# Block 0's last-row values turned on TensorE instead of through DRAM, and fillers between the late output-weight units

## The chip, the cores and the metric

The kernel runs on one core of one Trainium2 chip. A core has five engines with an instruction queue each: PE (TensorE, matrix multiplication), ACT (ScalarE), DVE (VectorE), POOL (GpSimd) and SP (SyncE, which issues most DMAs here). The data lies in SBUF, 128 partitions wide; TensorE writes into eight PSUM banks. The metric is the device time of one execution in microseconds (us), lower is better. Before the change it is 850.03 us, the median of three runs (849.67 to 851.71).

## The reference

A recurrent, memory-augmented attention layer with 32 heads, then a layer-normalised MLP. Shapes: 2048 tokens, width 512, 32 heads of 128, segments of 32 tokens, 8 memory rows.

```python
mem = mem0                                     # 8 x 512
for s in range(64):                            # 64 segments of 32 tokens
    xs = layernorm(x)[:, 32*s:32*s+32]
    h  = concatenate([mem, xs], axis=1)        # 40 rows
    q, k, v = (einsum('btd,dhe->bhte', h, W) for W in (Wq, Wk, Wv))
    scores = where(mask, einsum('bhqe,bhke->bhqk', q, k) * 128**-0.5, -1e9)
    o = einsum('bhqk,bhke->bhqe', softmax(scores), v)
    o = einsum('bhte,hed->btd', o, Wo)         # output projection
    mem = o[:, :8]                             # feeds the next segment
    outs.append(o[:, 8:])
h  = x + concatenate(outs, axis=1)
out = h + (gelu(layernorm(layernorm(h)) @ w1 + b1) @ w2 + b2)
```

The mask is causal, except that the 8 memory columns are open to all rows. Each segment needs the memory rows that the one before it made, so the 64 segments are one chain.

## The kernel before

Weights stay in SBUF: `WQ`, `WK`, `WV`, `WO` are 4 MB each, in bfloat16. They are loaded at the start: WV, WK, WQ as four DMAs of 1 MB, WO as sixteen of 256 KB, in this order on SP's queue. The Python list `chain` holds the order (`load` appends to it, and each DMA of the list comes behind the one ahead of it on SP).

The 40 rows of a segment are split. 32 of them, 8 memory rows and the first 24 token rows, are the "A" part (`hT`), which must wait for the memory. The last 8 rows of four successive segments together make a "B" part of 32 rows (`hB`), one per block of four segments, which needs no memory and is projected ahead of time. A projection pass (line 744, or 490 where the weights are kept) takes four 128-row steps; four matmuls of 512 columns run side by side in one step, in four column groups of the array. Passes come in halves r = 0 and 1, of 16 heads each.

The values of the B part come out as `VSB`: its partition stands for (column group j, segment s of the block, row t), and the four heads i of a group lie beside each other in the columns. For the product with the probabilities it is needed the other way round: in `VBD` the partition stands for (j, i, t), and the four segments s lie in the columns. Before the change `v_B_spread` (lines 832 to 844) does that through DRAM: four DMAs write `VSB` to the scratch tensor `v_last` (line 836), and four more read it back into `VBD` in 512-byte pieces (line 842). For block 0 these eight DMAs stand in the list of loads: `spread["out", 0]` behind WV and WK, `spread["in", 0]` behind WQ and the first two of WO's sixteen.

```python
chain[14:14] = spread["in", 0]
chain[8:8] = spread["out", 0]
```

`VSB` is a single buffer. Block 1's values (the entry `("B", "V", 1, ...)`) can be copied into it only when block 0's have been read. Such dependences are kept by tile: the class `Sched` records every operation with what it reads and writes, ranks them by estimated durations, and puts each engine's operations into an order; semaphore waits follow from it. TensorE's order is the one in which the code takes its operations: for segment 0 the hand-written list `START`, for the others `ORDER`. In `START`, `"X"` is the layer norm of token block 1 with its transposes, `"WO"` the output projection of segment 0, held back, and `("T", "WO", a, b)` takes its units a to b - 1. There are eight units (line 1009), and unit q needs the WO loads 2q and 2q + 1. Behind the last unit, DVE turns the result (line 1021) and adds halves into the memory columns of `hT` (line 1015), with which segment 1's projections begin.

TensorE's instruction stream is padded: `align` counts instructions and puts weight loads without a matmul (LDWEIGHTS, line 742) into the projections at a segment's start, so that the stream reaches a chosen place in its blocks of 256 (`PHASE`).

Of the kernel before, what the change touches and what calls it, by code (L numbers as in the profile page):

```python
# [44 lines left out]
START = (("B", "V", 0, (0, 6), (1, 7)), "V", "X", ("B", "V", 1, (0, 6), (1, 7)), ("B", "K", 0, (0, 4), (1, 6)), "K0", "K1", ("B", "K", 1, (0, 4), (1, 6)),  # L45
         ("B", "Q", 0, (0, 5)), "Q0", ("B", "Q", 0, (1, 4)), "Q1", "Z", "SC0", "SC1", ("B", "Q", 1, (0, 5)), "PV0", "PV1", "SA", "WO", ("T", "WO", 0, 3),
         ("B", "Q", 1, (1, 6)), ("T", "WO", 3, 8))


class Op:  # L50
# [394 lines left out]
P = 128  # L445
# [6 lines left out]
H = 32  # L452
# [9 lines left out]
MC, MR, MF = 1, 2, 3  # L462
# [45 lines left out]
def build_kernel(nc, A_x, A_mem0, A_Wq, A_Wk, A_Wv, A_Wo, B_w1, B_b1, B_w2, B_b2, out):  # L508
    scale = float(E) ** -0.5
    S = Sched(nc)  # L510
    st = contextlib.ExitStack()
    with st:
# [6 lines left out]
        WO = sb("WO", [P, H, D])  # L519
# [9 lines left out]
        ident = sb("ident", [P, P])  # L529
# [13 lines left out]
        VSB = sb("VSB", [P, 4, 2, E])  # L543
        VBD = sb("VBD", [P, 2, 4, 2, E])
# [14 lines left out]
        OTB = sb("OTB", [P, 2, H, 32])  # L559
# [55 lines left out]
        for sl in range(2):  # L615
            for i in range(4):
# [20 lines left out]
             reads=["maskA"], writes=["maskA"])  # L637
# [120 lines left out]
        def copy2(out, src, n, ps_=True, scale_=None):  # L758

            fast = 1.0 if ps_ else 0.5  # L760
            if scale_ is None:
                return {"act": (lambda e: e.copy(out, src), t_act(n, ps_)), "dve": (lambda e: e.tensor_copy(out, src), 0.16 + 1.042e-3 * n * fast)}  # L762
            return {"act": (lambda e: e.mul(out, src, scale_), t_act(n, ps_)),  # L763
                    "dve": (lambda e: e.tensor_scalar(out, src, scale_, None, ALU.mult), 0.16 + 1.042e-3 * n * fast)}
# [52 lines left out]

        def v_B_out(bk, r, bank):
            S.either(copy2(VSB[:, :, r, :], ps[bank][:, :].rearrange("p (i e) -> p i e", i=4), 512), reads=[("ps", bank)], writes=[("VSB", r)])
            if r == 1:  # L820
                v_B_spread(bk)

        def kq_B(bk, qk, r, bank, back=False):
# [4 lines left out]
        def v_B(bk, r, bank, back=False):  # L828
            one_pass(*pack_b(bk), WV, "WV", r, bank, cols_v, back)
            v_B_out(bk, r, bank)  # L830

        def v_B_spread(bk):

# [352 lines left out]
        for s in range(NS):  # L1186
# [109 lines left out]
            if s == 0:  # L1296

                for n in START:
                    if n[0] == "B":
                        _, what, b, *halves = n  # L1300
                        for r, bank in halves:
                            if what == "V":
                                v_B(b, r, bank)
                            else:
                                kq_B(b, "KQ".index(what), r, bank)
                    elif n[0] == "T":
                        S.take((0, n[1]), n[2], n[3])
# [157 lines left out]
```

## Time and profile before

| | us |
|---|---|
| median of three runs | 850.03 |
| the profiled execution's own time | 852.85 |
| its span, first to last instruction | 851.0 |
| PE busy | 801.9 (94%) |
| DVE, ACT, POOL busy | 566.5, 553.2, 265.3 |
| DMA packets, moved | 66615, 48.80 MB |

The span is the time between the first and the last instruction of the profiled execution; the rest of its time lies around it. All places below are given in us from the span's start. "PE" stands for matmuls, "PEld" for weight loads, "SPq" for the work of SP's queue, which issues DMAs; "PEclk" is the clock that was granted to TensorE, as a share of full speed. A row such as `[1.10 <-DMA WO<-in_A_Wo_dram]` says that the engine stood idle for 1.10 us before the instruction, and what ended the idleness. A segment takes about 10.5 us of the span in the steady part, and the first segment's work, with the loads, fills the first 52 us.

### The profile page before, as it was taken

The page shows a single profiled execution, that of the slowest core. Times are in us where ns is not written, and L with a number is a line of the kernel's source. Part 1 is how long each engine was busy: PE and PEld are TensorE (multiplying, and loading weights), DVE is VectorE, ACT ScalarE, POOL GpSimd, SP SyncE. Part 2 cuts the span into 40 slices and gives each one's busy share as a digit, 9 for nine tenths or more (in the row PEclk, how much of TensorE's full clock was granted, in tenths as well). Part 3 has the DMA queues.
Part 4 walks back from the last instruction along what each step waited for, and adds up shares of the span by engine and source line. Part 5 has one row for each costly group of instructions (what it writes and reads, how often), then busy time and mean ns, then how long its engine had stood idle before and what let it go on. Part 6 is the DMA issues. An engine that isn't in the chain of part 4 may idle for free.

```text
span 851.0 us, 47411 instructions
## 1 busy us (share of the span) xinstructions
PE 801.9 (94%) x20061; PEld 438.9 (52%) x22307; DVE 566.5 (67%) x1818; ACT 553.2 (65%) x1561; POOL 265.3 (31%) x686
## 2 busy tenths in 40 slices
PE   3668999999999999999999999999999998999998
PEld 1245555555555555555555555555555555544443
DVE  3257677878787878777778777777777776633111
ACT  2446777767776767777777777777777776742442
POOL 5023114242424242424242333323232313166200
PEclk9979999999999999999999999999999999999999
DMA  9961000110101010101010101010112121274100
GB/s 344 361 193 22 10 17 22 30 29 23 35 20 38 17 40 16 35 22 35 23 35 22 35 23 35 17 29 17 28 35 54 47 72 35 70 195 111 50 25 25
DMA packets 66615, 48.80 MB, mean 57 GB/s; under 512 B 29156, under 2 KB 62828, under 8 KB 66412
## 3 DMA queue, kind: packets, MB, share of 16 engines
q1 hardware_dynamic: 66080, 45.50, 18.4%
q8 instruction: 166, 2.72, 1.3%
q10 hardware_dynamic: 332, 0.27, 0.1%
q14 instruction: 37, 0.30, 0.1%
HBM read 31.34 MB, written 8.39 MB: 47 GB/s over the span
## 4 chain that ended last, share of the span: by engine, by line
PE 84%; DMA 5%; DVE 3%; POOL 3%; SPq 2%; issue 2%; ACT 1%; ACTq 0%; POOLq 0%; DVEq 0%
PE ps L744 36%; PE ps L1009 13%; PE ps L490 10%; PE quad L1357 6%; PE ps L1350 4%; PE ps L1036 4%; PE quad L919 3%; PE quad L977 3%; DMA oN<-opT 2%; PE quad L889 2%; PE ps L947 2%; PE ps L1164 2%; POOL opT L1050 2%; SPq L671 1%; DMA xr<-in_A_x_dram 1%
## 5 line engine op out<-in xcount | busy, mean ns | idle before, releaser
L762 ACT CAST OT<-quad 128x128 bf16<-128x128 f32 (+1 forms) x192 | 85.2, 444 | 144.8 <-PE quad L977 86.5
L970 POOL COPY BD<-PTA 32x192 bf16<-32x192 bf16 x256 | 88.8, 347 | 245.7 <-DVE PTA L966 222.7
L1009 PE MATMUL ps<-WO,OT 128*32 128x256 bf16 x4224 | 130.5, 275 | 4.5 <-DMA WO<-in_A_Wo_dram 3.7
L744 PE MATMUL ps<-WV,hT 128*32 128x512 bf16 x1780 | 132.7, 381 | 0.0
L744 PE MATMUL ps<-WQ,hT 128*32 128x512 bf16 x1796 | 123.3, 385 | 5.8 <-DVE hT L1015 4.4
L762 ACT CAST kq<-ps 128x512 bf16<-128x512 f32 x160 | 92.5, 588 | 34.0 <-PE ps L744 32.1
L1009 PEld LDWEIGHTS ps<-WO,OT 128*32 128x32 bf16 x4224 | 107.1, 97 | 12.9 <-DMA WO<-in_A_Wo_dram 3.7
L744 PE MATMUL ps<-WK,hT 128*32 128x512 bf16 x1544 | 108.8, 385 | 0.0
L763 ACT ACTIVATE kq<-ps 128x512 bf16<-128x512 f32 x160 | 92.6, 600 | 21.1 <-PE ps L744 20.8
L742 PEld LDWEIGHTS <-hT 128*32 128x32 bf16 x3942 | 65.8, 98 | 59.3 <-DVE hT L1015 30.8
L785 DVE STREAM_TRANSPOSE KALL<-kq 128x256 f32<-128x256 f32 x160 | 69.0, 438 | 24.1 <-ACT kq L762 14.6
L901 ACT ACTIVATE EC<-quad,nmc 128x64 f32<-128x64 f32 x252 | 77.2, 313 | 2.5 <-DVE nmc L897 0.2
L762 ACT CAST VS<-ps 128x512 bf16<-128x512 f32 x127 | 74.4, 586 | 0.0
L960 DVE TENSOR_REDUCE sma<-SA 128x8 f32<-128x256 f32 x64 | 26.9, 420 | 71.1 <-ACT SA L959 71.1
L744 PEld LDWEIGHTS ps<-WK,hT 128*32 128x32 bf16 x1544 | 45.9, 97 | 43.3 <-issue 24.6
L785 DVE STREAM_TRANSPOSE QT<-kq 128x256 f32<-128x256 f32 x128 | 55.7, 435 | 18.7 <-ACT kq L763 17.4
L806 POOL COPY ZC<-QTB 128x256 bf16<-128x256 bf16 x64 | 25.3, 396 | 122.8 <-PE quad L889 63.3
L1353 ACT ACTIVATE WQ<-ps,b1t 128x512 bf16<-128x512 f32 x42 | 28.9, 688 | 51.9 <-PE ps L1350 51.9
L919 PEld LDWEIGHTS quad<-PTC,VS 32*128 32x128 bf16 x2048 | 24.1, 91 | 74.0 <-ACT EC L901 24.3
L744 PEld LDWEIGHTS ps<-WV,hT 128*32 128x32 bf16 x1780 | 41.7, 95 | 33.4 <-issue 21.0
L744 PEld LDWEIGHTS ps<-WQ,hT 128*32 128x32 bf16 x1796 | 48.1, 95 | 19.8 <-issue 8.8
L490 PE MATMUL ps<-WK,hT 128*32 128x512 bf16 x504 | 51.0, 382 | 0.0
(150 smaller groups left out, 1489.8 us busy)
## 6 DMA issues: line engine op xcount, KB each, us to landing
WV<-in_A_Wv_dram SPq DMA_DIRECT2D x4, 1024.0 KB, 10.4
WK<-in_A_Wk_dram SPq DMA_DIRECT2D x4, 1024.0 KB, 18.8
v_last<-VSB SPq DMA_DIRECT2D x64, 64.0 KB, 2.6
WQ<-in_A_Wq_dram SPq DMA_DIRECT2D x4, 1024.0 KB, 11.8
WO<-in_A_Wo_dram SPq DMA_DIRECT2D x16, 256.0 KB, 7.3
VBD<-v_last SPq DMA_DIRECT2D x64, 64.0 KB, 2.5
h_mid<-xr SPq DMA_DIRECT2D x16, 128.0 KB, 1.8
WQ<-h_mid SPq DMA_DIRECT2D x4, 512.0 KB, 4.4
```

The source lines that it names most:

```text
L490: return e.add_instruction(mybir.InstMatmult(name="I-%d" % (4000000 + _kept[0]), engine=mybir.EngineType.PE, start_tensor_calc=start, stop ...
L742: e.ldweights(l, tile_position=(0, 32 * j))
L744: ins = e.matmul(o, l, m, start=(k == 0), stop=(k == DC - 1), tile_position=(0, 32 * j), skip_group_check=True)
L762: return {"act": (lambda e: e.copy(out, src), t_act(n, ps_)), "dve": (lambda e: e.tensor_copy(out, src), 0.16 + 1.042e-3 * n * fast)}
L763: return {"act": (lambda e: e.mul(out, src, scale_), t_act(n, ps_)), "dve": (lambda e: e.tensor_scalar(out, src, scale_, None, ALU.mult), ...
L785: S.op("dve", lambda e: e.transpose(out, src), reads=[("kq", i)], writes=[key], dur=t_dve(256) + 0.02)
L901: ins = e.activation(EC[:, r, sl, :], o[:, sl, :], ACTF.Exp, bias=nmc[:, r, sl:sl + 1], accum_out=smc[:, r, sl:sl + 1])
L919: e.matmul(quad[:, j, (4 * r + i) * 16:(4 * r + i) * 16 + 16], VS[rows, s % 3, r, i * E:(i + 1) * E], PTC[rows, r, c0:c0 + 16, i // 2], st ...
L970: S.narrow(S.op("pool", lambda e, j=j, rows=rows: e.tensor_copy(BD[rows, par, :, j, :, :], PTA[rows, :, 0:NA, :]), reads=["PTA"], writes=[ ...
L1009: ins = e.matmul(ps[bank][32 * j:32 * j + 32, 0:256], lhs(slot(h)), wo_cols(h, b), start=(k == 0), stop=(k == 15), tile_position=(0, 32 * ...
L1036: ins = e.matmul(ps[bank][32 * j:32 * j + 32, :], OTB[:, bk % 2, slot(8 * j + q), :], WO[:, 8 * j + q, :], start=(q == 0), stop=(q == 7), ...
L1357: S.op("pe", lambda e: e.matmul(quad[:, t, :], gT_of(k, fc)[:, t * P:(t + 1) * P], W2[:, fc, :], start=(fc == 0), stop=(fc == FC - 1)), re ...
```

## The change

Three things are edited.

First, block 0's `VSB` is turned on TensorE. `ZI`, a view of 608 columns in the second half of `OTB` (which is first written much later, by block 1), is cleared by POOL (one memset) and gets pieces of the identity matrix (one copy, behind `ident`). Slices of it, taken at shifted columns, are selection matrices. `v_B_turn` multiplies them with `VSB`: for each of the four segments s, four matmuls over i add up in PSUM, so 16 matmuls of 128 x 256 in two groups b, into the PSUM banks 0 and 1 of `quad`. One copy per group takes the result to `VBD`. It stands in `START` as `"S"`, behind `"X"`.

Second, block 0's eight DMAs go: `v_B_out` calls `v_B_spread` only for `bk > 0`, and the two lines on `chain` are deleted. The later blocks keep theirs.

Third, at the end of `START` the units of the output projection are cut differently around the last half of block 1's queries, and two fillers `("W", 7, 4)` come between units 5, 6 and 7. A filler is `warm(7, 4)`: four matmuls of `ident` with the first 512 columns of `WV` into PSUM bank 7, whose result nobody reads.

```diff
-START = (... "V", "X", ("B", "V", 1, (0, 6), (1, 7)), ...
+START = (... "V", "X", "S", ("B", "V", 1, (0, 6), (1, 7)), ...
          ... "SA", "WO", ("T", "WO", 0, 3),
-         ("B", "Q", 1, (1, 6)), ("T", "WO", 3, 8))
+         ("T", "WO", 3, 5), ("B", "Q", 1, (1, 6)), ("T", "WO", 5, 6), ("W", 7, 4), ("T", "WO", 6, 7), ("W", 7, 4), ("T", "WO", 7, 8))
...
-            if r == 1:
+            if r == 1 and bk > 0:
                 v_B_spread(bk)
...
+        ZI = OTB[:].rearrange("p a h t -> p (a h t)")[:, H * 32:H * 32 + 4 * (P + 24)].rearrange("p (s c) -> p s c", s=4)
+        S.op("pool", lambda e: e.memset(ZI, 0.0), writes=[("OTB", 1, sg) for sg in range(4)], dur=0.7)
+        S.op("pool", lambda e: e.tensor_copy(ZI[:, :, 24:].rearrange("p s (j c) -> p s j c", j=4)[:, :, :, 0:8], ident[:].rearrange("p (j s t) -> p s j t", j=4, s=4)),
+             reads=["ident"], writes=[("OTB", 1, sg) for sg in range(4)], dur=0.5)
+
+        def v_B_turn():
+
+            for b in range(2):
+                def f(e, b=b):
+                    for s in (2 * b, 2 * b + 1):
+                        for i in range(4):
+                            ins = e.matmul(quad[:, b, 256 * (s % 2):256 * (s % 2) + 256], ZI[:, s, 24 - 8 * i:24 - 8 * i + P], VSB[:, i].rearrange("p r e -> p (r e)"),
+                                           start=(i == 0), stop=(i == 3), skip_group_check=True)
+                    return ins
+                S.op("pe", f, reads=[("VSB", r) for r in range(2)] + [("OTB", 1, sg) for sg in range(4)], writes=[("ps", b)], dur=0.9, mode=MF, ni=16)
+                S.either(copy2(VBD[:, 0, 2 * b:2 * b + 2].rearrange("p s r e -> p (s r e)"), quad[:, b, :], 512), reads=[("ps", b)], writes=[("VBD", 0, b)])
...
+                    elif n == "S":
+                        v_B_turn()
...
-                chain[14:14] = spread["in", 0]
-                chain[8:8] = spread["out", 0]
                 chain += spread["out", 1] + spread["in", 1]
```

The order that results on SP's queue, at the start of the program. Before (`v_last` and `VBD` are the two transfers of the spread, `xr` the tokens of later blocks):

```order
L654 DMA WV<-in_A_Wv_dram 128x2x2048 x4
L654 DMA WK<-in_A_Wk_dram 128x2x2048 x4
L836 DMA v_last<-VSB 16x8x256 x4
L654 DMA WQ<-in_A_Wq_dram 128x2x2048 x4
L671 DMA WO<-in_A_Wo_dram 128x2x512 x2
L842 DMA VBD<-v_last 32x4x256 x4
L671 DMA WO<-in_A_Wo_dram 128x2x512 x14
L645 DMA xr<-in_A_x_dram 128x512 x3
L836 DMA v_last<-VSB 16x8x256 x4
```

And after the change:

```order
L654 DMA WV<-in_A_Wv_dram 128x2x2048 x4
L654 DMA WK<-in_A_Wk_dram 128x2x2048 x4
L654 DMA WQ<-in_A_Wq_dram 128x2x2048 x4
L671 DMA WO<-in_A_Wo_dram 128x2x512 x16
L645 DMA xr<-in_A_x_dram 128x512 x3
L853 DMA v_last<-VSB 16x8x256 x4
```

All weight loads now stand in one row, and the first DMA behind them that waits for a computed tile is block 1's `v_last`.

On PE, at the end of segment 0: `PTC,VBD` is the product with block 0's values, `KALL,QT` the scores of the A part, `WO,OT` the output projection (8 matmuls a unit), `WQ,hB` the last half of block 1's queries, `hT` the first projections of segment 1. Before:

```order
L923 MATMUL quad<-PTC,VBD 128x64 x4
L947 MATMUL ps<-KALL,QT 32x32 x32
L1009 MATMUL ps<-WO,OT 32x256 x24
L744 MATMUL ps<-WQ,hB 32x512 x16
L1009 MATMUL ps<-WO,OT 32x256 x40
L742 LDWEIGHTS hT x2
```

And after the change:

```order
L940 MATMUL quad<-PTC,VBD 128x64 x4
L964 MATMUL ps<-KALL,QT 32x32 x32
L1026 MATMUL ps<-WO,OT 32x256 x40
L744 MATMUL ps<-WQ,hB 32x512 x16
L1026 MATMUL ps<-WO,OT 32x256 x8
L713 MATMUL ps<-WV,ident 128x512 x4
L1026 MATMUL ps<-WO,OT 32x256 x8
L713 MATMUL ps<-WV,ident 128x512 x4
L1026 MATMUL ps<-WO,OT 32x256 x8
L742 LDWEIGHTS hT x2
```

Five units instead of three now stand ahead of the queries, and the fillers stand ahead of units 6 and 7. The 16 matmuls of the turn stand behind the transposes of `"X"` and ahead of block 1's values. From there on PE's order differs only in the number of the padding weight loads in segments 1 and 2; from segment 3 on it is the same.

On POOL, early in the program: `maskA`, `maskL` and `ident` are constants that PE needs first, `rst` is the layer norm's factor (the rows shown are token block 1's), `BD` a tile that is cleared. Before:

```order
L634 MEMSET maskA 128x256
L635 AFFINE_SELECT maskA<-maskA 128x8x24
L606 MEMSET maskL 128x32
L609 AFFINE_SELECT maskL<-maskL 128x8
L611 AFFINE_SELECT maskL<-maskL 128x16
L609 AFFINE_SELECT maskL<-maskL 128x8
L611 AFFINE_SELECT maskL<-maskL 128x16
L601 MEMSET ident 128x128
L602 AFFINE_SELECT ident<-ident 128x128
L685 TENSOR_SCALAR rst<-agg 128x1
L686 TENSOR_TENSOR rst<-rst,cneg 128x1
L640 MEMSET BD 128x1536
```

And after the change:

```order
L833 MEMSET OTB 128x608
L634 MEMSET maskA 128x256
L635 AFFINE_SELECT maskA<-maskA 128x8x24
L685 TENSOR_SCALAR rst<-agg 128x1
L686 TENSOR_TENSOR rst<-rst,cneg 128x1
L606 MEMSET maskL 128x32
L609 AFFINE_SELECT maskL<-maskL 128x8
L611 AFFINE_SELECT maskL<-maskL 128x16
L609 AFFINE_SELECT maskL<-maskL 128x8
L611 AFFINE_SELECT maskL<-maskL 128x16
L601 MEMSET ident 128x128
L602 AFFINE_SELECT ident<-ident 128x128
```

The memset of `ZI` (a part of OTB) and block 1's two `rst` operations have moved ahead of `maskL` and `ident`; the copy into `ZI` follows `ident`. On ACT's queue the load of token block 1 has moved from the fourth place to the second, and the two copies to `VBD` stand ahead of the copies of block 1's values.

More of the change, by code (lines that the diff above doesn't have):

```diff
@@ L44 @@
 OPEN_BANK = dict(K0=4, K1=5, Q0=6, Q1=7, V0=5, V1=4, SC0=6, SC1=7, SA=5, WO=4)
-START = (("B", "V", 0, (0, 6), (1, 7)), "V", "X", ("B", "V", 1, (0, 6), (1, 7)), ("B", "K", 0, (0, 4), (1, 6)), "K0", "K1", ("B", "K", 1, (0, 4), (1, 6)),
+START = (("B", "V", 0, (0, 6), (1, 7)), "V", "X", "S", ("B", "V", 1, (0, 6), (1, 7)), ("B", "K", 0, (0, 4), (1, 6)), "K0", "K1", ("B", "K", 1, (0, 4), (1, 6)),
          ("B", "Q", 0, (0, 5)), "Q0", ("B", "Q", 0, (1, 4)), "Q1", "Z", "SC0", "SC1", ("B", "Q", 1, (0, 5)), "PV0", "PV1", "SA", "WO", ("T", "WO", 0, 3),
-         ("B", "Q", 1, (1, 6)), ("T", "WO", 3, 8))
+         ("T", "WO", 3, 5), ("B", "Q", 1, (1, 6)), ("T", "WO", 5, 6), ("W", 7, 4), ("T", "WO", 6, 7), ("W", 7, 4), ("T", "WO", 7, 8))
 class Op:
```

## The prediction

> **What bounds the kernel now.** I read the page's clock row first, then the chain of waits, PE's waits and its order in time, and the busy time by stretches.
>
> ```profile
> PEclk9979999999999999999999999999999999999999
> ```
>
> Each digit is a 40th of the span, 21.3 us; only the third (42.6 to 63.8) falls to 7. Behind it the segments run evenly, so the place to read is the first 60 us. There the chain that ended last runs through DMAs:
>
> ```profile
> 20.60 7.06 DMA v_last<-VSB
> 27.75 1.97 SPq L842
> ...
> 45.41 6.78 DMA WO<-in_A_Wo_dram
> 52.32 0.64 PE ps L1009 x7
> ```
>
> The columns are start and us. The chain goes over both transfers of the spread and ends segment 0 with the landing of the last output weights, on which PE starts at once. PE's waits from 10 to 70 us (total, times, longest) say the same:
>
> ```profile
> PE ps L744 <- ACT VSB L762: 5.0, 1, 5.0
> PE ps L1009 <- DMA WO<-in_A_Wo_dram: 3.7, 4, 1.1
> ```
>
> The first is the single buffer: block 1's VSB copy had to wait until `v_last` had been written. PE in time:
>
> ```profile
> 38.84 0.62 PE L744 MATMUL ps<-WQ,hB 128*32 128x512 bf16 x8 [1.94 <-DMA WQ<-in_A_Wq_dram]
> ...
> 44.98 0.84 PE L1009 MATMUL ps<-WO,OT 128*32 128x256 bf16 x24
> 45.63 1.05 PE L744 MATMUL ps<-WQ,hB 128*32 128x512 bf16 x16
> 46.61 0.40 PE L1009 MATMUL ps<-WO,OT 128*32 128x256 bf16 x8
> 48.11 0.40 PE L1009 MATMUL ps<-WO,OT 128*32 128x256 bf16 x8 [1.10 <-DMA WO<-in_A_Wo_dram]
> ...
> 52.32 0.62 PE L1009 MATMUL ps<-WO,OT 128*32 128x256 bf16 x8 [0.71 <-DMA WO<-in_A_Wo_dram]
> 54.16 1.96 PE L744 MATMUL ps<-WQ,hT 128*32 128x512 bf16 x16 [1.21 <-DVE hT L1015]
> ```
>
> Units 4 to 7 each wait for weights; 1.84 us after the last one begins, segment 1 does. And the clock (columns: length, busy us and instructions of PE, PEld, DVE, ACT, POOL, granted clock, DMA share, GB/s):
>
> ```profile
> 42.13:45.55 3.42, 2.27 (x113) 1.52 (x108) 2.30 (x9) 2.79 (x13) 0.40 (x1) 1.00 1.10 349
> 45.55:48.96 3.41, 1.86 (x44) 0.74 (x32) 2.19 (x7) 1.01 (x2) 0.68 (x2) 1.00 1.10 350
> 48.96:52.37 3.41, 1.28 (x20) 0.42 (x24) 0.00 (x0) 0.00 (x0) 0.69 (x2) 0.55 0.89 276
> 52.37:55.79 3.42, 2.21 (x24) 1.36 (x64) 2.46 (x7) 0.00 (x0) 0.74 (x2) 0.50 0.57 169
> 55.79:59.20 3.41, 3.41 (x36) 2.32 (x88) 1.56 (x5) 1.56 (x3) 0.93 (x4) 0.50 0.43 98
> ```
>
> After the thin stretch that ends at 49, TensorE gets half its clock for 10.2 us, and keeps it while segment 1's projections are already running back to back.
>
> **Term 1: the DMAs that go.** The loads are limited by what the DMA engines move, not by issue (share over 1, GB/s in the last column):
>
> ```profile
> 27.70:35.30 7.60, 6.81 (x96) 3.41 (x96) 2.47 (x5) 3.45 (x6) 0.00 (x0) 0.78 1.02 412
> 35.30:42.70 7.40, 4.25 (x104) 1.76 (x96) 2.90 (x8) 4.41 (x14) 1.13 (x3) 1.00 1.12 275
> 42.70:49.00 6.30, 3.56 (x136) 2.04 (x128) 4.10 (x14) 3.23 (x11) 0.71 (x3) 1.00 1.10 350
> ```
>
> 1 MB weight loads run at 412 GB/s, WO at 350, and the stretch in which the read-back lands at 275. Issue times and times to landing of the last two WK loads, of the spread and of WO's first two:
>
> ```profile
> L654 SPq DMA_DIRECT2D WK<-in_A_Wk_dram x2: 1933/2196/2460, 4.7 to 6.6; - x2
> DMA to landing us min/median/max: 19.8/20.0/20.3
> ...
> L836 SPq DMA_DIRECT2D v_last<-VSB x4: 590/598/628, 18.7 to 20.6; - x4
> DMA to landing us min/median/max: 7.1/7.8/8.5
> ...
> L671 SPq DMA_DIRECT2D WO<-in_A_Wo_dram x2: 1462/1500/1537, 24.3 to 25.8; - x2
> DMA to landing us min/median/max: 15.0/15.3/15.5
> ...
> L842 SPq DMA_DIRECT2D VBD<-v_last x4: 1077/1214/1971, 27.7 to 32.1; - x4
> DMA to landing us min/median/max: 10.0/11.4/13.4
> ```
>
> WK is in at 6.6 + 20.3 = 26.9, `v_last` at 20.6 + 7.1 = 27.7: 0.8 us of the queue. WO's second load is in at 25.8 + 15.0 = 40.8, the read-back at 32.1 + 10.0 = 42.1: 1.3 us. So 2.1 us is the lower end. The whole way from 26.9 to the last WO landing (45.41 + 6.78 = 52.2) is 25.3 us. Without the spread it is 4 MB of WQ at 412 GB/s (4 x 1.049 MB, 10.2 us) and 4 MB of WO at 350 (12.0 us), 22.2 us: 3.1 less, since the 275 GB/s stretch also slows its neighbours. If WO came as fast as units 4 to 7 are spaced, (52.32 - 48.11) / 3 = 1.40 us a pair of loads, it is 11.2 us, and 3.9 less. I take 3.0, nearest to the sum over the whole way; ends 2.1 and 3.9.
>
> Is PE ready for that? WQ is then in at 26.9 + 10.2 = 37.1 instead of 38.8, so unit 0 can begin at 44.98 - 1.7 = 43.3. The units' weights land at 37.1 + 1.5 a unit: unit 3 at 43.1, unit 4 at 44.6, 5 at 46.1, 6 at 47.6, 7 at 49.1. Units 0 to 3 (0.22 us each, a third of 44.98 to 45.63) end at 44.2, unit 4 at 44.9, the queries (0.98, from 45.63 to 46.61) at 45.9, unit 5 at 46.4. So landings still decide, and moving two units ahead of the queries costs nothing.
>
> **Fillers.** Their nearest row is the MLP's full matmul:
>
> ```profile
> 803.62 1.03 PE L1350 MATMUL ps<-WQ,WK 128*128 128x512 bf16 x4
> ```
>
> Four take at most 1.03 us. A filler runs 46.4 to 47.4, ahead of unit 6's weights at 47.6; the next 47.9 to 48.9, ahead of 49.1. Cost nothing; the cover is WO's 1.5 us a unit. At half clock they take up to 2.06 us each, and units 6 and 7 run late: 46.1 + 0.4 + 2.06 + 0.4 + 2.06 + 0.4 = 51.5 for the end of unit 7 instead of 49.3. So 2 us is the upper end.
>
> **The turn.** 16 matmuls of half that width: at most 16 / 4 x 1.03 / 2 = 2.1 us on PE, 4.1 at half clock. It writes `quad`, so it waits for ACT's second copy of the transposes:
>
> ```profile
> 21.09 0.50 ACT L762 COPY hT<-quad 128x384 bf16<-128x384 bf16 x1
> ```
>
> That ends at 21.6. The turn then ends at 23.7, block 1's values (two half passes of 0.98) at 25.7, the first half of block 0's keys at 26.6; the second half needs WK, in at 26.9. On ACT the two VBD copies (512 columns, so 0.50 x 512 / 384 = 0.67 each) stand ahead of block 1's VSB copies, which the keys' second half needs; the first of these ends by 25.7. From 26.9 `START` has seven half passes and half of one, 7.4 us, until PE needs WQ's last load at 37.1: slack of 37.1 - 34.3 = 2.8 us. So the turn costs nothing. What was the 5.0 us wait for VSB ends at 26.9 on WK, and what is gained there is lost again ahead of WQ.
>
> **POOL and ACT at the start.**
>
> ```profile
> 13.34 0.61 PE L697 MATMUL quad<-ident,xn 128*128 128x128 bf16 x4 [2.06 <-DVE xn L687]
> ...
> 10.30 0.29 POOL L602 TENSOR_SCALAR_AFFINE_SELECT ident<-ident 128x128 bf16<-128x128 bf16 x1
> 11.05 2.31 POOL L685 TENSOR_SCALAR rst<-agg 128x1 f32<-128x1 f32 x1 [0.45 <-DVE agg L684]
> ...
> 13.96 1.38 POOL L640 MEMSET BD<- 128x1536 bf16 x1
> ```
>
> The memset ahead of `ident` is 608 / 1536 of 1.38, 0.55 us. `rst` has a second operation of 0.6 (13.36 to 13.96). If it need not wait, `ident` comes some 1.4 us later, at 12.0, still ahead of 13.34, where PE waits for `xn`. If token block 1 lands as before, POOL stands until 13.96, seven operations of 0.3 follow, and `ident` comes at about 16.1: PE 2.8 us late, as much as the slack. So 0; if a stretch at half clock comes on top, 1 us is the upper end. SP's other entries keep their order and come earlier.
>
> **Term 2: the clock.** The same four passes in segments 1 and 2 (first columns as above):
>
> ```profile
> 54.16:60.31 6.15, 6.15 (x68) 4.28 (x185) 3.20 (x10) 2.16 (x4) 1.99 (x5) 0.56 0.35 87
> 67.48:71.18 3.70, 3.69 (x65) 2.94 (x184) 2.76 (x8) 2.68 (x7) 2.18 (x6) 1.00 0.25 40
> ```
>
> At full clock segment 1 saves 6.15 - 3.70 = 2.45 us, whose weight loads for padding (185 and 184) cost nothing visible at full clock. After the change PE's gaps in the WO stage shrink to about 0.2 us; what stays is the 1.6 us between unit 7 and segment 1. Ends: 0 (the fall comes all the same) and 2.45. I take the upper: the stretch from 42.13, busy for 2.27 us, kept its clock, and the 3.41 us up to the end of unit 6 will hold 0.22 + 0.98 + 0.22 + 1.03 + 0.22 = 2.7.
>
> Here the Trainium skill is weighed (TensorE: Matmul & The Clock Gate, Part 1: The HAM clock gate): the clock halves after at least one idle window of about 3.4 us and returns after one busy one. Here it fell at 49 with no idle of PE over 1.1 us in the stretch ahead, so the measurement goes further than the rule; by the rule alone, no fall is left after the change, which is the same 2.45.
>
> **Sum.** 3.0 + 2.45 = 5.45 us. On the profiled execution that is 852.85 - 5.45 = 847.4 (its span 851.0 to about 845.6). The median of the runs lies 2.8 below that execution; the same saving gives 850.03 - 5.45 = 844.6.
>
> **Rivals.**
> 1. The fillers don't hold the clock: any 3.41 us that take in the 1.6 us gap have little more streaming than the stretch that ended at 49. One window at half clock in segment 1 costs 3.41 / 2 = 1.7: 846.3; all three, 847.0. For it: that row. Against it: afterwards PE is full, so one window is likelier than three. The Trainium skill (TensorE: Matmul & The Clock Gate, Part 1) says that this window runs freely, which would make it a matter of the single execution; one trace cannot show that.
> 2. The transfers were mostly hidden: only the 2.1 us, and no clock: 847.9, within 0.3% of before (0.3%, 2.5 us, is about what a measurement of this kernel can tell from no change).
> 3. Slower: the place of PE's instruction stream. 48 more instructions in segment 0 shift it. What a bad place does shows in one unit row of WO against another:
>
> ```profile
> 75.48 2.35 PE L1009 MATMUL ps<-WO,OT 128*32 128x256 bf16 x64
> 86.41 1.93 PE L1009 MATMUL ps<-WO,OT 128*32 128x256 bf16 x64
> ```
>
> 0.42 us more for the same 64 matmuls. If half of that, 0.2, came in each of 60 segments, it costs 12 us: 856.6. It outweighs the gain from 0.09 us a segment. Against it: the padding takes up the shift, and from segment 3 PE's order is unchanged.
>
> **Chances.** Main case 0.59 (844.6); rival 1 0.24; rival 2 0.09; rival 3 0.06; both terms at their upper ends, 843.7, 0.02. Faster: 0.59 + 0.24 + 0.02 = 0.85; same 0.09; slower 0.06. The range takes in the main case, rival 1 and the upper ends, with half of the runs' 2 us spread below: 843.4 to 847.6.
>
> **What would show it.** Right: no DMA of `v_last` ahead of WO; WQ's last landing near 37, the last unit's start near 49.2 and segment 1's near 51.1; PEclk 1.00 from 46 to 58 and 3.7 us from there to segment 1's scores; PE's wait for VSB gone. Wrong: a WO unit that waits for PE instead of DMA, half clock after 49, PE idle ahead of the turn longer than its slack, or longer segments after the third.

## The result, and the profile after

The changed kernel takes 851.24 us (median of 4 runs, 848.8 to 852.5); the kernel before, beside it on the same chip, 850.87 (4 runs, 849.67 to 851.95). The ratio is 1.0001, with a 95% interval of 0.9973 to 1.0029: no difference, where 5.45 us less were forecast. In a second measurement with 12 and 35 runs it is 852.41 against 852.72, ratio 0.999 (0.9972 to 1.0008). The profiled execution of the changed kernel took 851.16 us, with a span of 849.4.

What was to vanish has vanished. The page's clock row of the changed kernel no longer has a dip in the third slice:

```profile
PEclk9999999999999999999999999999999999999999
```

The weights land early. The view of WO's loads in the changed kernel (duration of the issue, first and last issue, then time to landing):

```profile
L671 SPq DMA_DIRECT2D WO<-in_A_Wo_dram x16: 557/824/2722, 21.0 to 41.9; - x16
...
DMA to landing us min/median/max: 6.9/7.6/16.8
```

The last one is in at about 41.9 + 6.9 = 48.8 us (its issue and the shortest time to landing); 49.1 was forecast, and before it was 52.2. PE in time, changed kernel (start, us, engine, line, operation; in brackets the idle time before and its end):

```profile
23.28 1.91 PE L843 MATMUL quad<-VSB,OTB 128*128 128x256 bf16 x16 [1.32 <-ACT hT L762]
...
37.03 1.04 PE L744 MATMUL ps<-WQ,hB 128*32 128x512 bf16 x8 [2.03 <-DMA WQ<-in_A_Wq_dram]
37.86 1.92 PE L744 MATMUL ps<-WQ,hT 128*32 128x512 bf16 x16
...
44.44 2.34 PE L1026 MATMUL ps<-WO,OT 128*32 128x256 bf16 x40
46.52 1.21 PE L744 MATMUL ps<-WQ,hB 128*32 128x512 bf16 x16
47.55 0.40 PE L1026 MATMUL ps<-WO,OT 128*32 128x256 bf16 x8
...
49.49 0.38 PE L713 MATMUL ps<-WV,ident 128*128 128x512 bf16 x1 [0.78 <-issue]
...
51.10 0.40 PE L1026 MATMUL ps<-WO,OT 128*32 128x256 bf16 x8
52.59 1.08 PE L744 MATMUL ps<-WQ,hT 128*32 128x512 bf16 x16 [1.09 <-DVE hT L1032]
```

No unit waits for weights any more: the last one starts at 51.10, 2.3 us behind its landing. Segment 1 starts at 52.59, 1.57 us earlier than before, where 3.0 were forecast. Units 0 to 4 take 2.34 us instead of the 1.1 that went into the forecast. The windows (length, then busy time and instructions of PE, PEld, DVE, ACT and POOL, granted clock, DMA share, GB/s) tell why. They are laid on the points at which the clock changes:

```profile
33.19:36.61 3.42, 1.45 (x24) 0.34 (x16) 1.10 (x3) 1.76 (x4) 0.00 (x0) 1.00 1.04 374
36.61:40.02 3.41, 2.96 (x40) 1.00 (x40) 0.45 (x1) 0.78 (x2) 0.74 (x2) 0.50 1.10 349
40.02:43.43 3.41, 1.65 (x68) 0.69 (x55) 2.19 (x9) 2.99 (x13) 0.40 (x1) 1.00 1.11 350
43.43:46.85 3.42, 2.93 (x96) 2.61 (x100) 1.96 (x7) 1.40 (x5) 0.00 (x0) 0.50 1.13 353
...
52.59:56.25 3.66, 3.56 (x64) 2.50 (x184) 3.25 (x10) 2.08 (x4) 1.58 (x4) 1.00 0.15 43
...
70.74:74.15 3.41, 1.66 (x73) 1.27 (x77) 2.77 (x10) 2.00 (x8) 0.47 (x2) 1.00 0.44 43
74.15:77.57 3.42, 3.16 (x54) 2.29 (x63) 1.25 (x5) 0.58 (x1) 0.58 (x2) 0.50 0.02 5
```

The clock now halves twice *ahead of* the fillers: in the window behind the wait for WQ, and again over units 0 to 4. From 46.85 on it is full, and the four passes that begin segment 1 take 3.66 us instead of 6.15, as forecast (3.70). But the gain does not stay. PE again, changed kernel, at the end of segment 1's scores, at the starts of segments 2 and 3, and in segment 2's output projection:

```profile
59.66 0.20 PE L964 MATMUL ps<-KALL,QT 128*32 128x32 bf16 x5 [1.23 <-issue]
...
64.37 1.45 PE L744 MATMUL ps<-WQ,hT 128*32 128x512 bf16 x16 [0.56 <-DVE hT L1032]
...
73.44 2.75 PE L1026 MATMUL ps<-WO,OT 128*32 128x256 bf16 x59 [0.78 <-issue]
...
77.21 1.21 PE L744 MATMUL ps<-WQ,hT 128*32 128x512 bf16 x16 [0.26 <-DVE hT L1032]
```

"Issue" is idle time in which the profile shows nothing that PE waited for: its next instruction is not there. Before the change, none of PE's waits in these two segments was put down to it. The second such stall thins out a window (70.74 to 74.15), and the next window runs at half clock. The kernel before, at the starts of segments 2 and 3:

```profile
67.48 1.43 PE L744 MATMUL ps<-WQ,hT 128*32 128x512 bf16 x16 [0.56 <-DVE hT L1015]
...
78.84 1.06 PE L744 MATMUL ps<-WQ,hT 128*32 128x512 bf16 x16 [0.55 <-DVE hT L1015]
```

Segment 3 starts at 77.21 instead of 78.84: of the lead of 3.11 us at segment 2, 1.63 is left. The profiled executions end 852.85 - 851.16 = 1.69 us apart.

### The profile page after: what moved, and what is told of

The parts are those of the page before. It is cut to its first block, busy times and chain, and to the rows that moved or that the text cites. A ratio compares the mean times of both kernels' runs of the same rounds, so it can differ in the third digit from the quotient of the medians.

```text
span 849.4 us, 47399 instructions
## 1 busy us (share of the span) xinstructions
PE 803.3 (95%) x20085; PEld 440.0 (52%) x22284; DVE 565.5 (67%) x1817; ACT 554.4 (65%) x1564; POOL 266.5 (31%) x688
## 4 chain that ended last, share of the span: by engine, by line
PE 86%; DMA 4%; DVE 3%; SPq 2%; issue 2%; POOL 1%; ACT 1%; POOLq 0%; DVEq 0%
PE ps L744 37%; PE ps L1026 14%; PE ps L490 10%; PE quad L1374 6%; PE ps L1367 4%; PE ps L1053 4%; PE quad L936 3%; PE quad L994 3%; DMA WQ<-in_A_Wq_dram 2%; SPq L654 2%; PE quad L906 2%; PE ps L964 2%; DMA oN<-opT 1%; PE ps L1181 1%; DVE TT L1038 1%
## 5 line engine op out<-in xcount | busy, mean ns | idle before, releaser
L742 PEld LDWEIGHTS <-hT 128*32 128x32 bf16 x3895 | 63.7, 96 | 59.1 <-DVE hT L1032 31.6
L785 DVE STREAM_TRANSPOSE QT<-kq 128x256 f32<-128x256 f32 x128 | 55.7, 435 | 17.5 <-ACT kq L763 16.1
```

What stands on the lines that cost most here:

```text
L742: e.ldweights(l, tile_position=(0, 32 * j))
L785: S.op("dve", lambda e: e.transpose(out, src), reads=[("kq", i)], writes=[key], dur=t_dve(256) + 0.02)
```

## The experiments

Two theories stood after the result; the first four forecasts call them A and B. A: the loads do land 3 us earlier and segment 1 has its clock, but the fillers stand on PE's path. B: the stalls put down to issue come each time, at the same places, and eat the gain. They do not exclude each other. Segment starts below are those of PE's first pass over `WQ,hT` in each profile, one profile for each version. In the kernel before they are 54.16, 67.48 and 78.84.

| kernel | median us | before, same session | ratio (95%) | segment 1 | 2 | 3 |
|---|---|---|---|---|---|---|
| changed, again | 852.41 | 852.72 | 0.9990 (0.9972 to 1.0008) | 51.73 | 63.78 | 76.76 |
| turn only | 851.55 | 852.72 | 0.9977 (0.9958 to 0.9997) | 50.42 | 64.43 | 74.88 |
| fillers doubled | 853.57 | 852.72 | 1.0007 (0.9989 to 1.0024) | 53.56 | 65.61 | 77.97 |
| fillers only | 852.77 | 852.72 | 1.0003 (0.9986 to 1.0019) | 55.41 | 67.34 | 77.82 |
| changed, no padding in segment 1 | 849.02 | 852.24 | 0.9962 (0.9942 to 0.9982) | 51.49 | 62.03 | 72.49 |
| turn only, no padding in segment 1 | 848.29 | 852.24 | 0.9954 (0.9936 to 0.9972) | 51.11 | 61.64 | 74.03 |
| before, no padding in segment 1 | 852.01 | 852.24 | 0.9993 (0.9973 to 1.0013) | 54.38 | 67.45 | 77.91 |
| changed, ten matmuls in the wait for WQ | 850.03 | 852.24 | 0.9971 (0.9956 to 0.9987) | 50.51 | 64.92 | 75.36 |
| both: ten matmuls, no padding | 847.43 | 853.12 | 0.9930 (0.9906 to 0.9954) | 50.91 | 61.53 | 71.99 |
| the same without the fillers | 849.23 | 853.12 | 0.9949 (0.9928 to 0.9969) | 50.59 | 62.65 | 73.11 |
| changed, 256 more padding loads | 855.75 (one run) | 853.12 | | 52.33 | 69.66 | 80.12 |

**The changed kernel again**, without an edit.

> The changed kernel once more, for a closer interval. Theory A: the loads do land 3 us earlier and segment 1 has its clock, but the eight filler matmuls run on PE's path (the last unit started 2.3 us behind its weights), so that segment 1 begins 1.6 us earlier and segment 2 3.1 us earlier; the rest of the program scatters by some 2 us from run to run. Then the mean should be 1 to 2.5 us under before. Theory B: the new place of PE's instructions brings stalls in which PE waits for nothing shown (0.78, 1.23 and 0.78 us in segments 0 to 2, none there before), each time; then the mean is that of before within 0.5 us, and this trace shows them at the same places.

Segment 1 starts at 51.73, segment 3 at 76.76, and it again has idle time put down to issue: 1.42 us in the first filler, 1.23 in segment 1's scores and 0.78 in segment 2's output projection. The result repeats, and so do the places of these stalls; the time, 0.3 us under the kernel before, is the one that theory B named. The clock does not repeat: here it halves only once ahead of the fillers, over units 0 to 4, and not behind the wait for WQ.

```profile
48.63 0.38 PE L713 MATMUL ps<-WV,ident 128*128 128x512 bf16 x1 [1.42 <-issue]
```

**The turn alone**, with the old order of the units and no fillers.

```diff
-         ("T", "WO", 3, 5), ("B", "Q", 1, (1, 6)), ("T", "WO", 5, 6), ("W", 7, 4), ("T", "WO", 6, 7), ("W", 7, 4), ("T", "WO", 7, 8))
+         ("B", "Q", 1, (1, 6)), ("T", "WO", 3, 8))
```

> The turn on TensorE without DMA, but no fillers, and the output-weight units cut as before (3, then the queries, then 5). Theory A: the last unit starts within 0.2 us of its weights' landing, near 48.9 us, and segment 1 at 50.5 to 50.8, 1.8 to 2 us ahead of the changed kernel; its passes are at half clock for one stretch or more (up to 6.2 us instead of 3.7). Time 1 to 3 us under before. Theory B: stalls of 0.7 us or more in segments 0 to 2 stay, and the time is that of before.

PE in time, the turn alone:

```profile
48.94 0.40 PE L1026 MATMUL ps<-WO,OT 128*32 128x256 bf16 x8 [0.73 <-DMA WO<-in_A_Wo_dram]
50.42 1.08 PE L744 MATMUL ps<-WQ,hT 128*32 128x512 bf16 x16 [1.08 <-DVE hT L1032]
...
58.37 0.66 PE L744 MATMUL ps<-WV,hT 128*32 128x512 bf16 x8 [1.65 <-issue]
```

Without the fillers the last unit waits for its weights again, and segment 1 starts 3.74 us earlier than before, 1.3 to 2.2 earlier than in the two executions with fillers. So the first term was sized right, and the fillers were on the path, as theory A has it; the time, 1.2 us under the kernel before, is at the low end of its forecast. In this execution segment 1 began at full clock even so; then it lost 1.65 us to issue and a window at half clock, and took 14.01 us.

**The fillers doubled**, eight matmuls each.

```diff
-... ("W", 7, 4), ("T", "WO", 6, 7), ("W", 7, 4), ("T", "WO", 7, 8))
+... ("W", 7, 8), ("T", "WO", 6, 7), ("W", 7, 8), ("T", "WO", 7, 8))
```

> The changed kernel with eight matmuls in each filler instead of four. Theory A (fillers on the path): segment 1 begins 1.7 us later than in the changed kernel (8 x 0.215), near 54.3, and the time is 1.7 us higher. If the fillers lay under the landing of the weights, as was predicted, at most 0.5 us.

Segment 1 starts at 53.56 (forecast 54.3), another 1.0 to 1.8 us later, for some 2 x 0.9 us of added matmuls; the time is 1.2 us above that of the changed kernel (forecast 1.7). If the fillers had been covered by the wait for weights, at least the first microsecond of this would have been, too.

**The fillers without the turn**: the kernel before with the last line of `START` from the changed one.

```diff
-          ("B", "Q", 1, (1, 6)), ("T", "WO", 3, 8))
+          ("T", "WO", 3, 5), ("B", "Q", 1, (1, 6)), ("T", "WO", 5, 6), ("W", 7, 4), ("T", "WO", 6, 7), ("W", 7, 4), ("T", "WO", 7, 8))
```

> The kernel before with the fillers and the new cut of the units, but with the transfers through DRAM. There the weights land later (52.2 us), so the fillers have cover: the last unit starts near 52.4 as before, segment 1 near 54.2, and by theory A its passes run at full clock, 3.7 us instead of 6.15: 2 to 2.5 us under before. If the clock isn't held by fillers, or theory B holds, the time of before.

The last unit starts at 53.91, where 52.4 was expected: the clock is at half from 43.1 to 53.4, and the two fillers take 1.89 and 1.42 us. Segment 1 starts at 55.41, 1.25 us later than before, but at full clock: segments 1 and 2 together take 22.41 us instead of 24.68. Segment 3 leads by 1.02 us, and no difference is left in the time. So in this execution the clock's gain exists and has the size of the second term (2.27 against 2.45), but the fillers' own delay eats half of it.

**No padding in segment 1.** The weight loads that do nothing are left out there (171); segment 2's fall from 119 to 34, and from segment 3 on every instruction is at its old place in its block. Nothing computed changes.

```diff
                 if owed > FETCH_N - SLIP:
                     owed = 0
+                if seg == 1:
+                    owed = 0
```

> The changed kernel with one table's effect switched off in segment 1: the 171 weight loads that do nothing and only move later instructions of TensorE to a chosen place are left out there, and segment 2's fall from 119 to 34, so that segments 3 and later stand where they stood. Nothing computed changes. Theory (TensorE is short of instructions in segment 1 once its passes run at the full clock: 715 and 647 instructions in segments 1 and 2, 256 fewer here): segment 1 takes 10.6 to 11.2 us instead of 11.77 and 12.05, its scores show no idle time put down to issue of 0.8 us or more, segments 1 and 2 together 22.5 to 23.5 us instead of 24.61 and 25.03, and the time falls by 1 to 2 us against the changed kernel. Rival A (the stall belongs to a transfer that crosses TensorE's instructions, not to their number): segments 1 and 2 together stay at 24.4 to 25.1 us, and the time within 0.5 us. Rival B (what is won there is waited for later, at a place that does not depend on TensorE): the start of segment 3 comes 1 to 2 us earlier and the time stays.

PE in time, changed kernel without padding in segment 1, at the starts of segments 1, 2 and 3:

```profile
51.49 1.05 PE L746 MATMUL ps<-WQ,hT 128*32 128x512 bf16 x16 [1.07 <-DVE hT L1034]
...
62.03 1.06 PE L746 MATMUL ps<-WQ,hT 128*32 128x512 bf16 x16 [0.56 <-DVE hT L1034]
...
72.49 1.06 PE L746 MATMUL ps<-WQ,hT 128*32 128x512 bf16 x16 [0.56 <-DVE hT L1034]
```

Segments 1 and 2 take 10.54 and 10.46 us, together 21.0 instead of 24.62, with no idle time put down to issue in either and no window at half clock. That is a larger gain than the theory had expected (22.5 to 23.5 us for the two), because the second window at half clock went along with the stall that had made it. The median is 3.2 us under the kernel before, where the changed kernel's was 0.3 under it. Rival A is out, since the number of instructions does count. So is rival B in the main, since most of what is won stays up to the end.

**The turn alone, no padding in segment 1**: the two edits above together.

> The turn on TensorE without the fillers (turn_only), and without the padding weight loads of segment 1 (187 fewer there, 69 fewer in segment 2). Theory (the turn is worth 3.7 us at the start of segment 1, the fillers only cost, and the padding eats what the clock gives): segment 1 starts at 50.0 to 50.8 us, takes 10.6 to 12.5 us instead of 14.00, segment 3 starts at 72.4 to 73.6 us instead of 74.89, and the time is 4 to 5.5 us under the kernel before: some 847.5 to 848.5 where that takes 852.7. Rival A (the stall does not depend on the number): segment 3 starts at 74.5 to 75.2 us and the time is that of turn_only, 851.5. Rival B (waited for later): segment 3 at 73 us, and the time still 851 to 852.

The time is close to the forecast (0.9954, 3.95 us under the kernel before; 4 to 5.5 were expected). Segment 1's start misses it (51.11, where 50.8 was the latest expected): the last unit waits for its weights until 49.64 in this execution. The profiled execution is the slowest of its twelve, at 852.38, and shows a stall of another kind in segment 2: DVE waits for POOL with the layer norm of a later token block, and PE behind it.

```profile
64.87 0.57 DVE L689 TENSOR_SCALAR xn<-xr,agg,rst 128x512 bf16<-128x512 bf16 x1 [2.48 <-POOL rst L688]
```

PE then waits 1.77 us, and segment 2 takes 12.39 us, so that segment 3's start (74.03) misses the forecast too. Segment 1 took 10.53.

**The kernel before, no padding in segment 1.** The same edit (192 fewer loads in segment 1, 64 in segment 2).

> The kernel before, without the padding weight loads of segment 1 (192 fewer there, 64 fewer in segment 2). Theory (the padding costs only where the passes run at the full clock; here segment 1 ran at half, and no idle time of its scores was put down to issue): segment 1 stays at 12.8 to 13.4 us, segments 1 and 2 together at 23.4 to 24.7, and the time within 1 us of the kernel before. Rival (the padding costs its instructions whatever the clock, 256 of them): segments 1 and 2 together 22 to 23 us, and the time 1.5 to 2.5 us under the kernel before; then the padding is a loss of its own that the change did not bring.

Segment 1 takes 13.07 us instead of 13.32, and segments 1 and 2 together 23.53 instead of 24.68; the ratio 0.9993 shows no gain, though its interval leaves room for 1.15 us. So it is not mainly the padding as such that costs. At half clock segment 1 hardly notices it; in the changed kernel, at full clock, 256 fewer instructions are worth 3.6 us up to segment 3.

**Ten matmuls in the wait for WQ.** Ten more matmuls whose result nobody reads, meant to hold the clock in that wait.

```diff
-... "Q0", ("B", "Q", 0, (1, 4)), "Q1", ...
+... "Q0", ("W", 7, 10), ("B", "Q", 0, (1, 4)), "Q1", ...
```

> The changed kernel with 10 more multiplications of 512 columns that nothing reads, between the first pass over the query weights that have landed and the second, in the 2.03 us that TensorE waits there for WQ; the fillers between the output-weight units stay. Theory (the clock halves in that wait and the thin stretch around it, so units 0 to 4 and the fillers run at half speed and TensorE comes 2.3 us behind its weights): units 0 to 4 take 0.22 us a pass instead of 0.42, the fillers are hidden behind the waits for WO, and segment 1 starts at 50.2 to 50.8 us as without fillers, instead of 52.59 and 51.74. Rival (the fillers are on the path by themselves, whatever the clock, or the clock halves before the added work): segment 1 starts at 51.7 us or later. The time by the theory 1 to 2 us under the changed kernel, unless segment 1 loses it to its instructions, which are 695 here.

PE in time and windows of this kernel:

```profile
34.13 2.11 PE L713 MATMUL ps<-WV,ident 128*128 128x512 bf16 x9 [0.16 <-issue]
...
49.02 0.40 PE L1026 MATMUL ps<-WO,OT 128*32 128x256 bf16 x8
50.51 1.08 PE L744 MATMUL ps<-WQ,hT 128*32 128x512 bf16 x16 [1.09 <-DVE hT L1032]
...
58.39 0.20 PE L964 MATMUL ps<-KALL,QT 128*32 128x32 bf16 x5 [1.15 <-issue]
```

```profile
36.42:39.83 3.41, 2.14 (x48) 0.76 (x40) 0.92 (x3) 1.56 (x4) 0.74 (x2) 1.00 1.10 351
39.83:43.24 3.41, 2.01 (x108) 1.17 (x112) 2.19 (x9) 2.76 (x13) 0.40 (x1) 1.00 1.10 348
...
56.90:60.31 3.41, 1.63 (x103) 0.96 (x90) 2.44 (x10) 1.86 (x8) 1.07 (x3) 1.00 0.00 0
60.31:63.72 3.41, 3.41 (x67) 2.36 (x59) 1.19 (x5) 0.92 (x3) 0.64 (x3) 0.50 0.21 43
```

In this execution the clock stays full from 20 us to 60, the fillers are hidden, the last unit starts at 49.02 (forecast 49.2) and segment 1 at 50.51, as without fillers. But no wait of more than 0.16 us for instructions stands in the fillers here either. So this run alone does not tell the half clock from the stall as what had put them on the path; the next one helps. Segment 1, still padded, then loses 0.81 and 1.15 us to issue and a window at half clock, and takes 14.41 us; the time is 2.2 us under the kernel before.

**Both together**: the ten matmuls in the wait, no padding in segment 1.

> The two cures together: the changed kernel with the 10 multiplications in the wait for the query weights, with its fillers, and without the padding weight loads of segment 1 (151 fewer there, segment 2's 119 become 14). Theory (the two losses are separate: the fillers on the path through the half clock, and TensorE short of instructions in the padded segment 1): segment 1 starts at 50.3 to 50.8 us, takes 10.5 to 10.8 us, segment 2 10.4 to 10.6, so segment 3 starts at 71.3 to 72.2 us where it started at 77.21 and 78.84 before, and the time is 4.5 to 6 us under the kernel before. Rival (one loss, which either cure removes alone): segment 3 at 72.5 us or later and the time that of the version without padding, 3.2 us under the kernel before. What each forecast has against it: single runs of one kernel differ by some 3 us through such stalls further on.

PE in time, this kernel: the last unit, and segments 1 and 3.

```profile
49.44 0.41 PE L1028 MATMUL ps<-WO,OT 128*32 128x256 bf16 x8
50.91 1.05 PE L746 MATMUL ps<-WQ,hT 128*32 128x512 bf16 x16 [1.07 <-DVE hT L1034]
...
71.99 1.06 PE L746 MATMUL ps<-WQ,hT 128*32 128x512 bf16 x16 [0.56 <-DVE hT L1034]
```

Its windows around units 0 to 4:

```profile
39.45:42.86 3.41, 1.79 (x68) 0.86 (x68) 2.53 (x10) 3.04 (x14) 0.95 (x3) 1.00 1.11 349
42.86:46.27 3.41, 3.21 (x100) 2.78 (x104) 1.97 (x6) 1.11 (x4) 0.00 (x0) 0.50 1.10 352
```

The ten matmuls did not hold the clock over units 0 to 4 here: they run at half clock, as in the changed kernel. Even so the last unit starts at 49.44, 0.3 us behind its landing (42.3 + 6.8 = 49.1), and there is no stall in the fillers. So half clock over units 0 to 4 alone does not put the fillers on the path.

Segment 3 leads by 6.85 us, and the time is 847.43 us (6 runs, 846.86 to 848.43) against 853.12: 5.7 us, or 0.7% (0.46 to 0.94), less. Of the versions tried it has the lowest median. It is faster in the median than the version without padding alone (ratio 0.9930 against 0.9962), but the two intervals overlap, and in the profile the difference up to segment 3 is only 0.5 us. Most of the recovery is the padding's.

**The same without the fillers.**

> The same without the fillers between the output-weight units and with the old order there: the turn, the 10 multiplications in the wait for WQ, no padding in segment 1. Theory (the fillers do nothing once the clock is held ahead of them): segment 1 starts at 50.0 to 50.8 us, segment 3 at 71.2 to 72.2 us, and the time is within 1 us of the version with fillers. Rival (the fillers hold the clock over the waits for WO, some 0.7 us each, and segment 1 falls to half clock without them): segment 1 takes 12 us or more, and the time is 1.5 us or more above the version with fillers.

Windows and PE in time, this kernel:

```profile
46.60:50.01 3.41, 1.61 (x44) 0.82 (x36) 0.98 (x3) 0.60 (x1) 1.36 (x4) 1.00 0.72 218
50.01:53.42 3.41, 2.83 (x28) 1.09 (x28) 2.69 (x9) 0.60 (x1) 1.58 (x4) 0.50 0.60 180
```

```profile
50.59 1.90 PE L746 MATMUL ps<-WQ,hT 128*32 128x512 bf16 x16 [1.06 <-DVE hT L1034]
```

Without the fillers segment 1 begins at half clock and takes 12.06 us instead of 10.62; the median is 1.8 us above the version with fillers (the intervals overlap). The theory that they do nothing falls, although its condition was not met: here too the clock is at half from 43.2 to 46.6, in spite of the ten matmuls. In these two profiles the fillers hold it over the late units. In the turn alone, segment 1 kept the full clock without them; the window of the late units (45.89 to 49.30) was busy for 1.91 us there, for 1.61 here.

**256 more padding loads in segment 1** of the changed kernel (427), so that the places from segment 2 on stay.

```diff
                 if owed > FETCH_N - SLIP:
                     owed = 0
+                if seg == 1:
+                    owed += FETCH_N
...
-                o.pad[0] = min(owed, PADS)
+                o.pad[0] = min(owed, 3 * PADS if seg == 1 else PADS)
```

> The changed kernel with 256 more padding weight loads in segment 1 (427 instead of 171), so that everything from segment 2 on stands at the place in its block of 256 instructions where it stood. Theory (the number of instructions in segment 1 is what TensorE waits for): segment 1 takes 13.5 us or more instead of 11.77 and 12.05, with idle time put down to issue of 1.5 us or more in sum. Rival (what counted was the place in the block, which is the same at the segment's end): 11.7 to 12.8 us. The loads' own time could also lengthen it: 174 padded passes' loads took 3.1 us on the weight-load side in segment 1 of the changed kernel; the idle time tells the two apart.

PE in time, this kernel, in the passes of segment 1:

```profile
56.21 0.60 PE L746 MATMUL ps<-WK,hT 128*32 128x512 bf16 x5 [2.02 <-issue]
...
60.26 0.68 PE L746 MATMUL ps<-WK,hT 128*32 128x512 bf16 x4 [1.13 <-issue]
```

Segment 1 takes 17.33 us: 10.54 without padding, 11.78 with 171 loads, 17.33 with 427. Of the last increase, 5.55 us, 3.15 are two stalls put down to issue in the middle of the passes, and a part is two windows at half clock behind them. The place at the segment's end was the same, so the number of instructions in the segment counts.

## Why the prediction was wrong

**Term 1, the DMAs that go: right.** The last WO landing came at 48.8 (forecast 49.1), PE went on behind WQ at 37.03 (37.1). In the five versions in which the last unit comes within 0.4 us of its weights, segment 1 starts 3.05 to 3.74 us earlier, within the stated ends of 2.1 and 3.9.

**The turn, POOL and ACT: right in what they cost.** The turn took 1.91 us. `ident` was ready at 14.86, between the two cases named (12.0 and 16.1), and PE's first pass began 2.15 us later than before (at 16.54, before at 14.39). That is inside the bound of 2.8, and PE still had to wait 2.03 us for WQ's last load.

**"Is PE ready for that?" and "Fillers" ("Cost nothing"): the first step that failed.** The step added up landings with PE at full clock and never short of instructions: unit 0 at 43.3, the queries' end at 45.9, the last unit near 49.2. In the changed kernel's profile these were 44.44, about 47.5 and 51.10, 2.3 us behind the last landing. Two things came in between. One is the clock: the window before 36.61, in which PE mostly waits for WQ, was busy for 1.45 us, and the next one ran at half clock; the same again at 43.43. The prediction had priced half clock for the fillers themselves (its upper end of 2 us), but looked for it behind the thin stretch, not ahead. The other is a wait for instructions in the first filler, 0.78 us, which the prediction put at nothing.

The profiles tell the two apart roughly. With half clock over units 0 to 4 alone, the last unit came 0.3 us behind its landing without such a stall (both edits together), 1.1 with 0.97 us of stalls (no padding) and 1.7 with 1.42 (the changed kernel again). So the stall stands on the path in full, and half clock over these units by itself is nearly hidden. What is left of the 2.3 us, some 1.2, goes with the earlier window at half clock, the one behind the wait for WQ. With the ten matmuls in that wait, it was absent in all three versions; without them it came in four of seven. No run changed the stall in the filler by itself.

**Term 2, the clock: the passes right, the sum wrong.** The passes took 3.66 us. The step that failed is "whose weight loads for padding cost nothing visible at full clock": it was read from the same four passes of segment 2, and the price falls due behind them. At full clock PE uses up its instructions faster than they come (the last section has the evidence). In the changed kernel this cost 1.23 us in segment 1 and 0.78 in segment 2, and through the thinned window one more window at half clock, up to 3.41 / 2 = 1.7 us. Without segment 1's padding these two segments are 3.6 us shorter; in the kernel before, which ran segment 1 at half clock, the same edit gained 1.15 us there and nothing that the time shows. In the six profiles that run segment 1 at full clock with its padding, the two segments take 24.41 to 25.03 us five times and 22.41 once (the fillers without the turn), where the kernel before took 24.68: mostly, the padding took all that the clock gave.

**The rivals.** Rival 1 (the fillers don't hold the clock) did not come: with them segment 1 began at full clock in all eight profiles, and without them, with the turn, once in three at half. Rival 2 (only part of the transfers counted) is out by the turn alone. Rival 3 had the right resource, PE's instruction stream, but put the loss at another place: not each of 60 segments, but two segments, by how many instructions they hold at full clock. From segment 3 on no loss repeats from segment to segment: from there to the end of the span, both kernels' profiles take 772.2 us (851.0 - 78.84 and 849.4 - 77.21).

With both edits together, 5.7 us were measured where the sum had 5.45. That these agree is partly luck: the lead at segment 3 was 6.85 us, part of it is padding that cost the kernel before something too, and the stall in the filler stayed away. The forecast was the sum of two gains with no rival for what the first 60 us wait for next.

## What to carry to other kernels

When a gain is a higher clock on some stage, ask what that stage was hiding at the old speed: here padding that was nearly free at half clock mostly cost what the clock gave. Fillers are free only if the engine reaches them on time, so work out its way there with the clock that it will have and the instructions that it needs, and not from landings alone. And a cost read from one stretch is a bound for that stretch alone: an instruction's price can fall due a few microseconds behind it.

## What the runs showed of the hardware

**The clock follows the busy share of a window, not only idleness.** In all thirteen profiles the recorded changes of the clock lie on a grid of 3.41 us. Of the 33 full-clock windows that began between 18 and 72 us and in which PE was busy for less than 1.90 us (0.33 to 1.89), 25 were followed by one at half clock; after the 144 with 1.92 us or more, none was. The eight that kept the clock were busy for 1.47 to 1.75 us, so the busy time of one window does not decide alone. Near 700 us the clock also fell behind windows with up to 2.08 us. At half clock, eight windows with 1.27 to 2.80 us were followed by another at half clock, and the 23 with 2.73 us or more by a full one, so the bounds overlap a little; a matmul's end is modelled. The Trainium skill (TensorE: Matmul & The Clock Gate, Part 1: The HAM clock gate) has the clock fall after an idle window of that length. Here 22 of the 25 windows ahead of a fall were busy for 1.21 us or more, so they held no idle time over 2.2 us; the measurement decides.

Where the grid lies differs from execution to execution. In four of the seven profiles with the turn and without the ten matmuls, one window, begun at 33.2 to 33.6 us, took in most of a wait of 2.0 us for WQ's last load and was busy for only 1.21 to 1.45 us, and the next ran at half clock. In the other three the border lay at 35.3 to 35.6, the wait was shorter (1.1 to 1.7 us), its window was busy for 1.55 to 1.75 us, and the clock fell only behind the window after it.

**PE's instructions are a resource.** They come in transfers of their own. The page of the changed kernel, in the section on DMA queues (packets, MB, share):

```profile
q8 instruction: 166, 2.72, 1.3%
```

PE has 20085 matmuls, 22284 weight loads and 329 recorded semaphore instructions, 42698 in all: 256 for each of 166.8 packets. The page counts 166, of 16 KB each, so they are PE's. The times of these packets are in the traces, and they tell what ends the stalls. In the thirteen profiles PE has 129 waits of 0.25 us or more put down to issue (behind the first 5 us). All 129 ended 1.20 to 1.62 us after the end of such a packet; of PE's matmuls in general, 9% begin at such a distance. And all stand at one place in PE's count of instructions: 191 to 216 in a block of 256, 122 of them at 191 to 197. So these stalls, 0.25 to 2.02 us long, are waits for the next 256 instructions, those in the fillers and in the later segments too. No two of these packets began less than 3.23 us apart. A run that delays a packet by itself was not made.

**Single executions scatter.** The kernel before took 849.32 to 857.91 us in the 35 runs of one measurement. From segment 3 to the end of the span, the thirteen profiles take 771.9 to 776.7 us, so the lead at segment 3 is not always the lead at the end: 6.35 us of the version without padding are 852.85 - 847.0 = 5.85 at the end, 4.81 of the turn alone without padding only 0.47. Profiles show waits for instructions of 0.3 to 1.2 us at changing segments up to the end; why one segment has such a wait in one execution and not in the next stays open.
